# More weight loads under way, no idle products in a stretch of the front, and other keys for the MLP's units in a planned RWKV and MLP kernel

## The chip, the cores and the metric

The kernel runs on one core of one Trainium2 chip. The metric is the device time of one execution in microseconds (us); the median of the runs counts. The core has five engines with an instruction queue each: TensorE (PE) for products and transposes, with its weight loads shown apart as PEld, VectorE (DVE), ScalarE (ACT), GpSimd (POOL), and SyncE (SP), which here issues nearly all DMAs.

## The reference

Two stages in fp32. The first is RWKV attention over 4 batches, 8 heads, 768 steps, head size 48:

```
for t in range(S):
    cur = einsum('bhd,bhe->bhde', u * k[t], v[t])
    y[t] = einsum('bhd,bhde->bhe', r[t], state + cur)
    state = w * state + einsum('bhd,bhe->bhde', k[t], v[t])
```

The second takes y as x of 4 x 768 x 384:

```
h  = x.transpose(0, 2, 1) @ U @ V          # over the 768 steps, rank 32
u  = x + h.transpose(0, 2, 1)
out = u + relu(u @ w_ch1) @ w_ch2          # 384 -> 1536 -> 384
```

U, V and both weights reach the chip as 64-bit floats; the kernel reads them as pairs of 32-bit words.

## The kernel before

**Attention.** Each batch is cut into six chunks of 128 steps, n = 0 to 23. A chunk scales k by a table of powers of w (ks, from the table tabf, which is turned by the transposes pt_tabf of back), turns r and k with transposes on PE (ptr, ptk, then rT and kT), makes the score products kT x rT (bank_tr and bank_sc, eight pairs), masks them on DVE (am), and adds am x v and rT x state S into pav. A state product psu gives the next S. dv and dg hold the term with u. Chunks of batch 0 (the front) are cut by `f_scores`, `f_state` and `f_out`; later ones by `a_chunk` or `a_part`.

**MLP.** Behind a batch's attention come the product with U and V (Gs), u in a high and a low part (uTh, uTl), and units of work m_1 and m_2, each for a tile of tokens and a quarter of the 1536 columns. A half-unit is nine products of 128x384 into p: three tiles of weight times high, low and correction parts. m_1 reads w1s and uTh, uTl; ACT makes hh = relu(p) (L1298) and DVE the rest hl (L1299); m_2 reads w2s and hh, hl. The nine products have one line, L384, since a helper records them.

**Weights.** `unit` holds a weight tile: `load` issues its DMA, and converting from 64-bit words takes ACT (L597, L619), DVE (L600, L603) and a split into a high part by ACT (L637) and a low part by DVE or POOL (L638). A list `landing` holds the loads that were made; each load is tied to the landing of the one AHEAD places before it, so that no more than AHEAD are under way. SP issues them in order, and a load that waits holds up what stands behind it.

**The order.** A planner (`Plan`) fixes the order on every engine. Each step has a key, given by `at(t, f)`: the front's chunks stand EACH = 4.5 apart, the MLP's units PER apart from T0 on, the blocks of later batches by begin[b]. The planner walks through the steps by keys with a model of each operation's time, its engine and the readiness of its inputs, and always starts the best one next. Its PE part reckons with half or full clock (`clock`). Where PE would stand idle in plan time, it puts in idle products ident x ident of 128x128 into the bank wake (`woken`, line 384 in the profile), the number of which comes from the model. Prices are given with each operation, such as 950 ns for the score products and 500 for the outer ones.

The lines that the change touches in the load:

```
big_one = len(parts) == 1 and name != "u"
before = landing[-AHEAD] if big_one and len(landing) >= AHEAD else None
...
tc.add_manual_dep(mine[0].ins, before[0][0].ins.name, ...)
```

and the place at which idle products are put in:

```
until = t - 150 - (...)
while self.pe_end(x, begin.ways[0][1], 0, False) < until:
    self.woken.append((x, filler))
```

Of the kernel before, what the change touches and what calls it, by code (L numbers as in the profile page):

```python
# [47 lines left out]
class Plan:  # L48
# [19 lines left out]
    USED = 0.36  # L68

    BACKLOG = 0.3  # L70
    NEXT = 1500
    YIELD, YIELDS, NEAR = 2, 140000, 100

# [47 lines left out]
    def clock(self, t):  # L121
        w = int(t // self.WINDOW)
        for x in range(len(self.clocks), w + 1):
            self.clocks[x] = 1.0 if self.work.get(x - 1, 0) > self.USED * self.WINDOW else 0.5
        return self.clocks[w]

    def pe_end(self, t, ns, share, note=True):
# [27 lines left out]
    def schedule(self):  # L155
# [50 lines left out]
        while left:  # L206
# [36 lines left out]
                cands[w[0]] = [c for c in cands[w[0]] if c[0] is not o]  # L243
            if e == "PE":
                for begin, end, filler in self.wakes:
                    if begin.end is None or end.end is not None:
                        continue

                    x = free[e]
                    until = t - 150 - (min(self.SPARE * (t - x), 600) if self.clock(x) == 1 else 0)  # L250
                    while self.pe_end(x, begin.ways[0][1], 0, False) < until:
                        self.woken.append((x, filler))
                        x = self.pe_end(x, begin.ways[0][1], 0.8)
                        tiled = False
                    t = max(t, x)
                if o.tiled != tiled:
                    t, tiled = t + self.MODE, o.tiled
                ns = self.pe_end(t, ns, 0.65 if tiled else 0.85) - t
# [61 lines left out]
def rwkv_moe(ctx: ExitStack, tc: tile.TileContext, r, k, v, w, u, U, V, w1, w2, out):  # L320
# [65 lines left out]
    def pe(ns, fn, w_, r_, tiled=False, dk=0.0):  # L386
        return op("PE", ns, fn, w_, r_, tiled=tiled, dk=dk)
# [154 lines left out]

    wide = U.dtype == I64

    AHEAD = 3
    HOLD = 6
    landing = []

# [366 lines left out]
    def in_turn(*lists):  # L915
        for k_ in range(max(map(len, lists))):
            for l in lists:
                if k_ < len(l):
                    l[k_]()
# [74 lines left out]
    def f_scores(n):  # L994

        rT, kT = trs[n]
        abs_[n] = [bank(t, f"pab_{n}_{j}") for j, t in enumerate(AB)]

        def product(q, j):
            rows = head_rows(j)  # L1000
            return nc.tensor.matmul(abs_[n][j].t[:, q * C:(q + 1) * C], lhsT=kT.t[rows, q, :], rhs=rT.t[rows, q, :],  # L1001
                                    start=True, stop=True)
        pe(950, lambda: in_turn(*([lambda q=q, j=j: product(q, j) for q in range(NP)] for j in range(2))), abs_[n], [rT, kT],
           tiled=True)
        ams[n] = []
        for j in range(2):
            am = xbuf([128, NP, C], F32, "bl", 5, f"am_{n}_{j}")
            ams[n].append(am)
            on_dve(512, lambda e, am=am, j=j: e.tensor_tensor(am.t, abs_[n][j].t.rearrange("p (q t) -> p q t", q=NP),
                                                              before_.unsqueeze(1).broadcast_to([128, NP, C]), ALU.mult),  # L1010
                   [am], [abs_[n][j]])
# [32 lines left out]
    def f_out(n):  # L1044

        vt, vb = vs[n]
        rT = trs[n][0]
        avp[n] = [bank(t, f"pav_{n}_{j}") for j, t in enumerate(("av", "mm"))]

        def inner(q, j, i):  # L1050
            return nc.tensor.matmul(avp[n][j].t[i * C2:(i + 1) * C2, q * D:(q + 1) * D],  # L1051
                                    lhsT=ams[n][j].t[:, q, i * C2:(i + 1) * C2], rhs=vt()[:, 2 * q + j, :],
                                    start=(q == 0), stop=(not n and q == NP - 1), skip_group_check=True)

        def outer(q, j, i):
            rows = head_rows(j)
            return nc.tensor.matmul(avp[n][j].t[i * C2:(i + 1) * C2, q * D:(q + 1) * D], lhsT=rT.t[rows, q, i * C2:(i + 1) * C2],  # L1057
                                    rhs=St[n, 0].t[rows, q, :], start=False, stop=(q == NP - 1), skip_group_check=True)
        for j in range(2):
            pe(500, lambda j=j: in_turn(*([lambda q=q, i=i: inner(q, j, i) for q in range(NP)] for i in range(2))),  # L1060
               [avp[n][j]], [ams[n][j], *vb], tiled=True)
        if n:
            pe(500, lambda: in_turn(*([lambda q=q, j=j, i=i: outer(q, j, i) for q in range(NP)] for i in range(2) for j in range(2))),
               avp[n], [rT, St[n, 0]], tiled=True)
        x = xs[n] = xbuf([128, DM], F32, "x", NX, f"x_{n}")
        dv = dvs[n]
        for j in range(2):
            def pair(ap, j=j):
                return ap.rearrange("p (q j) d -> p q j d", j=2)[:, :, j]
            on_dve(192, lambda e, j=j, pair=pair: e.tensor_tensor(  # L1070
                pair(by_head(x.t)), avp[n][j].t[:, :NP * D].rearrange("p (q d) -> p q d", q=NP), pair(dv.t), ALU.add),
                [(x, j)], [avp[n][j], dv])
# [388 lines left out]
    def at(t, f):  # L1461
        steps.append((t, len(steps), f))

    T0, PER = 40.0, 1.85
    UV, GX, UVC = -84.9, (3, 33.0), (25.0, 33.0)
    EARLY, LEAD = 4, 12.0
    FRONT, EACH = 9.0, 4.5
# [41 lines left out]
    def attention(b, t0, per, lead, step):  # L1509
        n0 = b * NCH  # L1510
        for c in range(NCH):
            n = n0 + c
            t = t0 + per * c
            prepare(n, t - per - lead if c else t - 2 * lead)
            if front(n):
                at(t - SC, lambda n=n: f_scores(n))
                at(t - SU_, lambda n=n: f_state(n))
                at(t, lambda n=n: f_out(n))
                at(t - 1, lambda n=n: a_dg(n))
                if c >= GX[0]:  # L1520
                    at(max(t + per - 0.05, GX[1] + 0.1 * c), lambda n=n: gx.append(c_gx(*(range(n + 1) if n == GX[0] else [n]))))
                continue
            if c == 0:
                at(t - 5, lambda n=n: a_first(n))
            if merged(n):
                at(t, lambda n=n: a_chunk(n))
            else:
                at(t, lambda n=n: a_part(n, 0))
                at(t + per / 2, lambda n=n: a_part(n, 1))
            at(t - 0.1, lambda n=n: a_dg(n))  # L1530
        return t0 + per * NCH
# [4 lines left out]
    for b in range(B):  # L1536
        n0 = b * NCH
        last = b + 1 == B
        t = begin[b]
        if b:  # L1540
            t0, per = ((begin[b - 1] + 34, 8.0), (begin[b - 1] + 5, 10.0))[b > 1]
            for c in range(NCH):
                at(t0 + per * c - per - 16, lambda n=n0 + c: a_load(n))
            for c in range(0, NCH, 3):
                if turned(n0 + c):
                    continue
                for i in (1, 3, 0, 2):
                    at(t0 + per * c - per - 18 + 0.1 * i, lambda n=n0 + c, i=i: (a_load_blocks(n, i, 0), a_load_blocks(n, i, 1)))
            end = attention(b, t0, per, 5.0, 0)
        at(end, lambda b=b: c_g(b))  # L1550
        if b == 0:
            at(end + 0.9, lambda: again.append(pe(220, refill, [wk2], [xs[NCH - 1], V3])))
            at(end + 1, lambda: c_xu(0, 0))
            at(end + 1.5, lambda: again.append(pe(0, lambda: None, [wk2], [(uT[0, 0][1], NCT - 1)])))
            for i in range(TPB):
                at(t + 2 + 0.1 * i, lambda i=i: c_x(0, 1, i))
            at(t + 3, lambda: c_xu(0, 1))
        else:
            if inside(b, 0):
                for i in range(3):  # L1560
                    at(end + 0.1 + 0.1 * i, lambda b=b, i=i: c_x(b, 0, i))
                at(end + 1, lambda b=b: c_xu(b, 0))
            else:
                for i in range(TPB):
                    at(end + 0.2 + 0.1 * i, lambda b=b, i=i: (c_u(b, i), c_store(b, i)))
                for ct in range(NCT):
                    at(end + 1 + 0.1 * ct, lambda b=b, ct=ct: c_blocks(b, 0, ct))
                    at(end + 5 + ct, lambda b=b, ct=ct: c_turn(b, 0, ct))
            for i in (3, 4, 5):
                at(end + (8 if b > 1 else 2) + 0.3 * (i % 3), lambda b=b, i=i: (c_u(b, i), c_store(b, i, parts=2 if b > 1 and i > 3 else 1)))  # L1570
        for ct in range(NCT if b else 0):
            at(t + 2 + ct, lambda b=b, ct=ct: c_blocks(b, 1, ct))
            at(t + 16 + ct, lambda b=b, ct=ct: c_turn(b, 1, ct))
        for j, f in enumerate(mlp_units(b)):
            at(t + PER * j, f)
# [42 lines left out]
```

## Time and profile before

| what | value |
|---|---|
| median of 3 runs | 403.54 us (403.44 to 403.96) |
| the profiled execution | 403.42 us |
| its span, first to last instruction | 401.7 us |
| granted clock of PE, mean | 0.996 |
| PE busy | 393.9 us, 98% |
| DVE, ACT, POOL busy | 262.6, 139.2, 100.3 us |
| products p of 128x384 | 1728 |
| MB moved by DMA | 45.28 |

The span is what the trace covers; 1.72 us of the execution lie outside it. The share of busy time is an average over stages. In the front (up to about 36 us) all engines work on batch 0's attention; from 42 us the MLP's products fill PE, with blocks of later batches' attention between them; from 309 us on there is nothing but the MLP. A row with several instructions shows them as one ("x4"), with the time from the first's start to the last's end.

### The profile page before, as it was taken

The numbers are of one execution on the slowest core, as the hardware profiler recorded it, in microseconds if no ns is written. First come the engines' busy times: TensorE is split into PE (matmuls) and PEld (weight loads), VectorE is DVE, ScalarE is ACT, GpSimd is POOL, SyncE is SP. The second block draws the span as 40 slices with busy tenths as digits, with TensorE's granted clock in tenths as the row PEclk, the third lists the DMA queues.
The fourth block names the chain that finished last, engine by engine and source line by source line (L and its number), as shares of the span: only waits on it lengthen the run. The fifth ranks groups of instructions, "written<-read, shape, count | busy, mean of one in ns | idle before, by whom it ended". The sixth has DMA issues, their size and how long they took to land.

```text
span 401.7 us, 11702 instructions
## 1 busy us (share of the span) xinstructions
PE 393.9 (98%) x4872; PEld 380.4 (95%) x4872; DVE 262.6 (65%) x559; ACT 139.2 (35%) x376; POOL 100.3 (25%) x147
## 2 busy tenths in 40 slices
PE   7999999999999999999999999999999999999994
PEld 7888999999999999999999999999999999999994
DVE  4789998899999868976784596776424552121122
ACT  3688869437361332222112331202112221111110
POOL 2881223266736042231230150431000110000000
PEclk9999999999999999999999999999999999999998
DMA  9988699879578586864786858310104620001001
GB/s 150 178 231 237 118 270 182 192 181 220 88 120 193 82 184 104 164 101 82 146 156 98 188 117 143 75 19 12 51 2 74 145 77 2 0 0 62 2 0 64
DMA packets 189994, 45.28 MB, mean 113 GB/s; under 512 B 174701, under 2 KB 188398, under 8 KB 189934
## 3 DMA queue, kind: packets, MB, share of 16 engines
q1 hardware_dynamic: 186382, 43.28, 53.0%
q10 hardware_dynamic: 3552, 1.18, 1.3%
q8 instruction: 40, 0.66, 0.7%
q14 instruction: 20, 0.16, 0.1%
HBM read 36.77 MB, written 7.67 MB: 111 GB/s over the span
## 4 chain that ended last, share of the span: by engine, by line
PE 94%; DVE 3%; DMA 1%; SPq 0%; issue 0%; ACT 0%
PE p L384 75%; PE pav L898 2%; PE pav L904 2%; PE bank_tr L1001 2%; PE pav L1051 2%; DMA ld<-in_r_dram 1%; PE bank_tr L858 1%; PE bank_sc L858 1%; PE ptr L807 1%; PE pav L883 1%; PE bank_tr L872 1%; PE bank_tr L1165 1%; PE bank_sc L872 1%; PE pav L1057 1%; PE psu L1023 1%; PE bank_tr L807 1%
## 5 line engine op out<-in xcount | busy, mean ns | idle before, releaser
L384 PE MATMUL p<-uTh,w1s 128*128 128x384 f32 x576 | 148.6, 338 | 0.0
L384 PE MATMUL p<-w2s,hh 128*128 128x384 f32 x576 | 119.1, 337 | 0.1
L1298 ACT ACTIVATE hh<-p 128x384 fp32r<-128x384 f32 x96 | 47.1, 490 | 207.3 <-PE p L384 206.7
L1299 DVE SCALAR_TENSOR_TENSOR hl<-p,hh 128x384 fp32r<-128x384 f32 x96 | 53.2, 554 | 93.3 <-ACT hh L1298 92.2
L384 PEld LDWEIGHTS p<-uTh,w1s 128*128 128x128 f32 x576 | 103.1, 188 | 1.1 <-DVE w1s L638 0.3
L384 PEld LDWEIGHTS p<-w2s,hh 128*128 128x128 f32 x576 | 100.8, 188 | 1.1 <-DVE w2s L638 0.4
L384 PE MATMUL p<-uTl,w1s 128*128 128x384 f32 x288 | 96.6, 335 | 0.0
L384 PE MATMUL p<-w2s,hl 128*128 128x384 f32 x288 | 66.7, 335 | 0.0
L384 PEld LDWEIGHTS p<-uTl,w1s 128*128 128x128 f32 x288 | 54.0, 188 | 0.2 <-DVE uTl L1229 0.2
L384 PEld LDWEIGHTS p<-w2s,hl 128*128 128x128 f32 x288 | 51.5, 188 | 0.0
L1275 POOL TENSOR_TENSOR uTl<-ut,uTh 128x384 fp32r<-128x384 f32 x8 | 8.1, 1018 | 74.9 <-ACT uTh L1274 74.8
L759 POOL MEMSET ks<- 128x128 f32 x24 | 4.7, 205 | 66.1 <-PE bank_tr L872 65.3
L898 PE MATMUL pav<-ldv,am 64*64 64x48 f32 x288 | 20.2, 219 | 0.0
L904 PE MATMUL pav<-S,rT 48*64 48x48 f32 x528 | 19.6, 218 | 0.0
L898 PE MATMUL pav<-vsw,am 64*64 64x48 f32 x288 | 18.4, 218 | 0.0
L898 PEld LDWEIGHTS pav<-ldv,am 64*64 64x64 f32 x288 | 17.9, 134 | 0.0
L904 PEld LDWEIGHTS pav<-S,rT 48*64 48x64 f32 x528 | 17.9, 135 | 0.0
L1339 DVE TENSOR_TENSOR x<-p,x 128x384 f32<-128x384 f32 x30 | 14.9, 548 | 3.6 <-PE p L384 3.3
L898 PEld LDWEIGHTS pav<-vsw,am 64*64 64x64 f32 x288 | 17.2, 134 | 0.0
L597 ACT ACTIVATE raw_w<-raw_w 128x384 int32<-128x384 uint8 x23 | 13.1, 569 | 8.7 <-DMA raw_w<-in_moe_w_ch_dram 8.7
L796 POOL TENSOR_TENSOR kT<-kT,tabT 112x512 f32<-112x512 f32 x10 | 12.9, 1290 | 11.8 <-DVE kT L794 6.3
L769 POOL TENSOR_TENSOR dv<-ldr,ldk 128x384 f32<-128x384 f32 x14 | 14.2, 1016 | 5.6 <-DVE x L1103 3.0
(189 smaller groups left out, 593.8 us busy)
## 6 DMA issues: line engine op xcount, KB each, us to landing
raw_w<-in_moe_w_ch_dram SPq DMA_DIRECT2D x24, 384.0 KB, 5.0
out_dram<-x SPq DMA_DIRECT2D x21, 192.0 KB, 2.2
ldr<-in_r_dram SPq DMA_DIRECT2D x20, 192.0 KB, 3.3
ldk<-in_k_dram SPq DMA_DIRECT2D x20, 192.0 KB, 3.8
ldv<-in_v_dram SPq DMA_DIRECT2D x20, 192.0 KB, 4.0
bl<-in_r_dram SPq DMA_DIRECT2D x79, 48.0 KB, 2.4
bl<-in_k_dram SPq DMA_DIRECT2D x79, 48.0 KB, 2.4
ub<-ud SPq DMA_DIRECT2D x15, 192.0 KB, 2.9
```

The lines of the kernel that those rows point to most:

```text
L384: return nc.tensor.matmul(*args, **kw)
L597: nc.scalar.activation(word(0), byte(), AF.Copy, scale=7.49 / 255)
L769: on_either(384, lambda e, a_=a_, b_=b_: e.tensor_mul(dv.t, a_()[:, :, :D], b_()[:, :, :D]), w_, r_, only="POOL" if front(n) else None)
L796: on_either(512, lambda e: e.tensor_mul(subs(xT.t[:PD]), subs(xT.t[:PD]), table(i)), [xT], [tabT])
L807: nc.tensor.transpose(pt.t[:PD, q * C:(q + 1) * C], src().rearrange("p h d -> p (h d)")[:, q * PE_:q * PE_ + PD], ident_)
L858: return [lambda q=q, i=i: nc.tensor.matmul(pt.t[(i ^ j) * C2:(i ^ j) * C2 + C2, q * C2:(q + 1) * C2], lhsT=kT.t[rows, q, i * C2:(i + 1) * ...
L898: return nc.tensor.matmul(to(q, j, i), lhsT=am[j].t[half, q, :], rhs=vsw[n].t[half, q, :] if j else vt()[half, 2 * q, :], start=((i == 1 i ...
L904: return nc.tensor.matmul(to(q, row, i), lhsT=rT.t[rows, q, i * C2:(i + 1) * C2], rhs=St[n, i].t[rows, q, :], start=False, stop=((alone or ...
L1275: on_either(384, lambda e: e.tensor_tensor(ul.t[:, ct, :], ut.t, f32(uh.t[:, ct, :]), ALU.subtract), [(ul, ct)], [ut, (uh, ct)])
L1298: on_act(384, lambda: nc.scalar.activation(hh.t, pt.t[:, :TB], AF.Relu), [hh], [pt])
L1299: on_dve(384, lambda e: e.scalar_tensor_tensor(hl.t, pt.t[:, :TB], 0.0, f32(hh.t), ALU.max, ALU.subtract), [hl], [pt, hh])
L1339: on_dve(384, lambda e, x=x, pt=pt: e.tensor_tensor(x.t, pt.t[:, :DM], x.t, ALU.add), [x], [pt])
```

## The change

Six edits, all to numbers or conditions of the planner but for the first:

- AHEAD goes from 3 to 5: five weight loads may be under way.
- A new QUIET = 7000, 9500: where plan time lies between these, no idle products are put in.
- `clock` counts on the full clock from its third step on, whatever the work before.
- The score products are priced at 1000 instead of 950, the outer products at 520 instead of 500.
- PER goes from 1.85 to 1.95: the units of the MLP have keys further apart.
- The diagonal dg of the front's chunks has its key at t - 0.1 instead of t - 1, and the blocks of batches 2 and 3 begin at begin[b - 1] + 6 instead of + 5.

```
+    QUIET = 7000, 9500
...
-            self.clocks[x] = 1.0 if self.work.get(x - 1, 0) > self.USED * self.WINDOW else 0.5
+            self.clocks[x] = 1.0 if x > 1 or self.work.get(x - 1, 0) > self.USED * self.WINDOW else 0.5
...
-                    if begin.end is None or end.end is not None:
+                    if begin.end is None or end.end is not None or self.QUIET[0] < t < self.QUIET[1]:
...
-    AHEAD = 3
+    AHEAD = 5
...
-        pe(950, lambda: in_turn(*([lambda q=q, j=j: product(q, j) for q in range(NP)] for j in range(2))), abs_[n], [rT, kT],
+        pe(1000, lambda: in_turn(*([lambda q=q, j=j: product(q, j) for q in range(NP)] for j in range(2))), abs_[n], [rT, kT],
...
-            pe(500, lambda: in_turn(*([lambda q=q, j=j, i=i: outer(q, j, i) for q in range(NP)] for i in range(2) for j in range(2))),
+            pe(520, lambda: in_turn(*([lambda q=q, j=j, i=i: outer(q, j, i) for q in range(NP)] for i in range(2) for j in range(2))),
...
-    T0, PER = 40.0, 1.85
+    T0, PER = 40.0, 1.95
...
-                at(t - 1, lambda n=n: a_dg(n))
+                at(t - 0.1, lambda n=n: a_dg(n) )
...
-            t0, per = ((begin[b - 1] + 34, 8.0), (begin[b - 1] + 5, 10.0))[b > 1]
+            t0, per = ((begin[b - 1] + 34, 8.0), (begin[b - 1] + 6, 10.0))[b > 1]
```

A line more stands in the changed kernel from line 71 on, so its numbers are one higher. On PE, the order near the start of the program, where the first chunk is turned and its scores are made, is in the kernel before:

```order
L384 MATMUL wake<-ident 128x128
L807 MATMUL ptr_138<-ident,ld_93 112x128 x4
L384 MATMUL wake<-ident 128x128 x2
L488 MATMUL pt_tabf<-ident,back 128x112 x4
L384 MATMUL wake<-ident 128x128
L1001 MATMUL bank_tr<-rT_160,kT_150 128x128
L1001 MATMUL bank_sc<-rT_160,kT_150 128x128
```

and in the changed one:

```order
L385 MATMUL wake<-ident 128x128
L808 MATMUL ptr_138<-ident,ld_93 112x128 x4
L489 MATMUL pt_tabf<-ident,back 128x112 x4
L1002 MATMUL bank_tr<-rT_158,kT_149 128x128
L1002 MATMUL bank_sc<-rT_158,kT_149 128x128
L1002 MATMUL bank_tr<-rT_158,kT_149 128x128
```

Three idle products are gone, two ahead of pt_tabf and one ahead of the scores. Over the whole program PE has no other instruction more or less; behind the first chunk the two orders are alike up to about 63 us of the trace before, as are those of DVE, ACT and POOL up to about 52 us.

On SP, the first weight loads, with the semaphores that each waits for (a load of DMAHW1 to DMAHW7 is tied to the landing of an earlier one on that semaphore; w1_0 is the first quarter of w_ch1), before:

```order
L572 DMA raw_w1_0_497<-in_moe_w_ch1_dram 128x3x256 [waits DMAHW1_49]
L572 DMA raw_w2_0_503<-in_moe_w_ch2_dram 128x768 [waits DMAHW2_49]
L572 DMA raw_w1_1_505<-in_moe_w_ch1_dram 128x3x256 [waits DMAHW3_49]
L572 DMA raw_w2_1_599<-in_moe_w_ch2_dram 128x768 [waits DMAHW4_49,DMAHW1_49]
L572 DMA raw_w1_2_615<-in_moe_w_ch1_dram 128x3x256 [waits DMAHW5_49,DMAHW2_49]
L572 DMA raw_w1_3_647<-in_moe_w_ch1_dram 128x3x256 [waits DMAHW6_49,DMAHW3_49]
```

and in the changed kernel:

```order
L573 DMA raw_w1_0_486<-in_moe_w_ch1_dram 128x3x256 [waits DMAHW1_49]
L573 DMA raw_w2_0_500<-in_moe_w_ch2_dram 128x768 [waits DMAHW2_49]
L573 DMA raw_w1_1_502<-in_moe_w_ch1_dram 128x3x256 [waits DMAHW3_49]
L573 DMA raw_w2_1_511<-in_moe_w_ch2_dram 128x768 [waits DMAHW4_49]
L573 DMA raw_w1_2_528<-in_moe_w_ch1_dram 128x3x256 [waits DMAHW5_49]
L573 DMA raw_w1_3_589<-in_moe_w_ch1_dram 128x3x256 [waits DMAHW6_49,DMAHW1_49]
```

The second semaphore is gone from the fourth and fifth load, and the sixth waits for the first.

On DVE, late in the conversion of the weights, between the last low part of a weight (w2s_11) and a rest hl of the MLP (hl_0_1_8, batch 0, second tile of tokens), before:

```order
L638 TENSOR_TENSOR w2s_11_2248<-raw_w2_11_1737,w2s_11_2248 128x384
L1299 SCALAR_TENSOR_TENSOR hl_0_0_11_2261<-p1_0_0_11_2221,hh_0_0_11_2252 128x384
L794 STREAM_TRANSPOSE rT_13_2265<-bl_12_0_1454 128x256
L794 STREAM_TRANSPOSE rT_13_2265<-bl_12_2_2018 128x256
L794 STREAM_TRANSPOSE kT_12_2065<-bl_12_3_2105 128x256
L794 STREAM_TRANSPOSE kT_13_2239<-bl_12_3_2105 128x256
L760 TENSOR_TENSOR ks_12_2215<-ldk_12_2241,tab_922 128x8x48
L1299 SCALAR_TENSOR_TENSOR hl_0_1_8_2296<-p1_0_1_8_2244,hh_0_1_8_2287 128x384
```

and in the changed kernel:

```order
L639 TENSOR_TENSOR w2s_11_2239<-raw_w2_11_1720,w2s_11_2239 128x384
L797 TENSOR_TENSOR rT_13_2237<-rT_13_2237,tabT_900 112x512
L1300 SCALAR_TENSOR_TENSOR hl_0_0_11_2291<-p1_0_0_11_2226,hh_0_0_11_2286 128x384
L795 STREAM_TRANSPOSE rT_14_2295<-bl_12_0_1622 128x256
L795 STREAM_TRANSPOSE kT_12_2198<-bl_12_3_2151 128x256
L795 STREAM_TRANSPOSE kT_13_2230<-bl_12_3_2151 128x256
L797 TENSOR_TENSOR kT_12_2198<-kT_12_2198,tabT_900 112x512
L761 TENSOR_TENSOR ks_12_2204<-ldk_12_2241,tab_919 128x8x48
L770 TENSOR_TENSOR dv_12_2322<-ldr_12_2232,ldk_12_2241 128x384
L797 TENSOR_TENSOR kT_13_2230<-kT_13_2230,tabT_900 112x512
L770 TENSOR_TENSOR dv_12_2322<-dv_12_2322,ub_136 128x384
L1300 SCALAR_TENSOR_TENSOR hl_0_1_8_2339<-p1_0_1_8_2310,hh_0_1_8_2332 128x384
```

Four more rows stand between the two: three products with the table tabT and two for dv came from POOL, one transposition went elsewhere. Over the whole program DVE has six rows more, 720 for 714.

## Rows read from the trace of the kernel before

**Rows 1.** The page's first part: busy time of each engine, its share of the span and its instructions; and the second part's line of DVE, the busy share in tenths of 40 slices.

```profile
PE 393.9 (98%) x4872; PEld 380.4 (95%) x4872; DVE 262.6 (65%) x559; ACT 139.2 (35%) x376; POOL 100.3 (25%) x147
...
DVE  4789998899999868976784596776424552121122
```

**Rows 2.** The windows: each stretch in us, then its length, the busy us of PE, PEld, DVE, ACT and POOL with the instructions, then the granted clock, the share of DMA and GB/s.

```profile
9.70:13.10 3.40, 3.40 (x72) 3.09 (x70) 2.95 (x6) 1.30 (x5) 2.51 (x3) 1.00 1.09 208
...
36.00:42.00 6.00, 5.66 (x42) 4.83 (x43) 5.45 (x12) 5.17 (x14) 1.02 (x1) 1.00 0.82 166
42.00:52.00 10.00, 9.91 (x56) 8.98 (x55) 10.00 (x23) 8.06 (x18) 2.80 (x7) 1.00 0.70 129
52.00:96.00 44.00, 44.00 (x539) 42.84 (x538) 39.52 (x86) 27.66 (x72) 19.13 (x25) 1.00 0.89 204
96.00:134.00 38.00, 38.00 (x658) 36.27 (x657) 37.22 (x78) 16.66 (x51) 18.82 (x22) 1.00 0.74 143
...
309.00:396.50 87.50, 87.49 (x505) 87.16 (x503) 27.17 (x48) 16.14 (x34) 3.02 (x3) 1.00 0.15 39
```

**Rows 3.** The chain of work that ended last, in order of time: start us, us, what.

```profile
49.82 1.85 PE p L384 x9
...
79.29 3.33 PE p L384 x18
82.62 0.44 PE bank_tr L807 x4
83.05 1.57 PE p L384 x9
84.62 0.44 PE bank_tr L807 x4
...
309.09 87.41 PE p L384 x504
```

**Rows 4.** What PE waited for between 13 and 52 us: us in total, times, longest us.

```profile
PE pu L384 <- DVE Gs L1188: 0.3, 1, 0.3
```

**Rows 5.** The timeline of the front: start us, us, engine, line, operation, out<-in, and in brackets the idle time before.

```profile
6.22 1.10 PE L807 MATMUL ptr<-ident,ld 128*112 128x128 f32 x4 [0.31 <-DMA ld<-in_r_dram]
...
6.64 0.62 ACT L508 COPY back<-pw 112x512 f32<-112x512 f32 x1 [3.46 <-DVE pw L503]
...
7.12 1.06 PE L384 MATMUL wake<-ident 128*128 128x128 f32 x4
...
7.36 1.13 DVE L820 SCALAR_TENSOR_TENSOR rT<-ptr,wif,pw 112x128 f32<-112x128 f32 x4
...
7.97 0.95 PE L488 MATMUL pt_tabf<-ident,back 112*128 112x112 f32 x4
...
8.72 0.66 PE L384 MATMUL wake<-ident 128*128 128x128 f32 x2
8.96 0.48 ACT L490 COPY tabf<-pt_tabf 128x384 f32<-128x384 f32 x1 [1.61 <-PE pt_tabf L488]
...
9.31 0.57 PE L1001 MATMUL bank_tr<-rT,kT 48*128 48x128 f32 x1
...
9.68 0.31 PE L1001 MATMUL bank_tr<-rT,kT 48*128 48x128 f32 x1
...
9.83 0.27 PE L1001 MATMUL bank_tr<-rT,kT 48*128 48x128 f32 x1
...
10.39 0.27 PE L1001 MATMUL bank_tr<-rT,kT 48*128 48x128 f32 x1
...
10.60 0.65 PE L807 MATMUL ptr<-ident,ld 128*112 128x128 f32 x4
10.70 0.69 DVE L1009 TENSOR_TENSOR am<-bank_tr,before 128x512 f32<-128x512 f32 x1 [0.20 <-PE bank_sc L1001]
```

**Rows 6.** The timeline where the next idle products stand, behind the second chunk's scores.

```profile
14.72 1.28 PE L384 MATMUL wake<-ident 128*128 128x128 f32 x10
14.74 1.00 POOL L760 TENSOR_TENSOR ks<-ld,tabf 128x384 f32<-128x384 f32 x1
...
15.84 0.61 PE L807 MATMUL ptk<-ident,ks 128*112 128x128 f32 x4
```

**Rows 7.** The first weight loads: the timeline's row of SP, the DMA issues of 23 to 26 us and of 28 to 33.5 us (number, KB each, median us from issue to landing), and the timeline's rows of ACT for the first and the fourth conversion.

```profile
23.80 9.71 SPq L572 DMA_DIRECT2D raw_w<-in_moe_w_ch_dram  x8
...
raw_w<-in_moe_w_ch_dram SPq DMA_DIRECT2D x3, 384.0 KB, 5.3
...
raw_w<-in_moe_w_ch_dram SPq DMA_DIRECT2D x5, 384.0 KB, 4.3
...
30.70 0.57 ACT L597 ACTIVATE raw_w<-raw_w 128x384 int32<-128x384 uint8 x1
...
33.41 0.59 ACT L597 ACTIVATE raw_w<-raw_w 128x384 int32<-128x384 uint8 x1
```

**Rows 8.** Groups of DVE instructions by line over the whole span: busy us, mean ns of one, idle time before.

```profile
L794 DVE STREAM_TRANSPOSE kT<-bl 128x256 f32<-128x256 f32 x30 | 12.6, 426 | 0.8 <-DMA bl<-in_k_dram 0.8
...
L769 DVE TENSOR_TENSOR dv<-dv,ub 128x384 f32<-128x384 f32 x14 | 10.0, 718 | 0.0
...
L796 DVE TENSOR_TENSOR kT<-kT,tabT 112x512 f32<-112x512 f32 x5 | 3.3, 668 | 0.0
L769 DVE TENSOR_TENSOR dv<-ldr,ldk 128x384 f32<-128x384 f32 x6 | 3.3, 542 | 0.0
```

## The prediction

> **What bounds the kernel now.** I read the page's shares first: TensorE (PE) is busy 393.9 of 401.7 us, VectorE (DVE) 262.6 [rows 1]. The windows then say where the rest lies [rows 2]: from 52 us to the end of the products PE has no idle time that a row shows (44.00 of 44, 38.00 of 38, 87.49 of 87.50), while the stretches 36 to 42 and 42 to 52 leave 0.34 and 0.09 idle, with DVE busy 10.00 of 10 in the second. The chain of waits gives PE's pace [rows 3]: nine products of 128x384 take 1.57 us, and the last 504 take 87.41, 0.173 each; a group of transposes between two units (82.62 + 0.44 = 83.06) leaves no gap. One piece at 49.82 takes 1.85 for nine, 0.28 over the pace. The waits of PE name one other, 0.3 us on Gs [rows 4]. So behind 52 us the time is PE's own work. An edit can gain by less work on PE, by an earlier arrival at 52 us, or by a better pace in the front; it loses by a new wait behind 52 us.
>
> The front is read from the timeline [rows 5]. Four transposes take 1.10 us at 6.22 and 0.65 at 10.60, and eight pairs of score products start 0.37 apart at first and 0.11 apart from 9.83: PE runs at the lower of its two levels until about 9.7 us and at the higher one after it. The granted clock reads 1.00 (2.4 GHz) over the stretch, so the durations are what I go by.
>
> **The idle products that go.** In the order they are one row of two ahead of pt_tabf and one ahead of the scores; the trace shows each product as two rows. pt_tabf needs back, which ACT ends at 6.64 + 0.62 = 7.26, and PE is through with ptr at 6.22 + 1.10 = 7.32; it starts at 7.97, behind the four idle rows from 7.12 [rows 5]. Without them it starts at about 7.31, 0.66 earlier, and tabf with it (8.96 to 8.30). The scores need rT, which ends at 7.36 + 1.13 = 8.49, and start at 9.31 behind two idle rows from 8.72; without these they start at about 8.55, since pt_tabf then ends at 7.31 + 0.95 = 8.26. That is 0.76 earlier, but they run at the lower level for longer. I keep the moment of the step at 9.7, take twice the 0.11 for a pair ahead of it and 0.37 for the first: pairs start at 8.55, 8.92, 9.14, 9.36, 9.58, then 9.76, 9.87, 9.98 in place of 10.39. The gain at the last pair is 10.39 - 9.98 = 0.41, with the rounding of a pair 0.42. The next ptr starts 0.21 behind it (10.60 to 10.18), am on DVE at 10.28 for 10.70.
>
> Does the 0.42 get through? At 14.72 five idle products follow, which stay in both orders; they end at 15.84, when ks (14.74 + 1.00 = 15.74 on POOL) is just there [rows 6]. POOL's ks hangs on the table tabf, which comes 0.66 earlier, so PE's own order decides there, and the shift stays. From there to about 52 us the orders of PE, DVE, ACT and POOL are the same in both programs; the DVE work of 37 to 52 us starts when PE delivers, so it shifts with PE. Behind 52 us PE has nothing to wait for, so the shift goes to the end. **Term: -0.42 us.** Bounds: 0 (if the front gives it back at 14.72) and -0.76 (if the step of the clock moves with the scores).
>
> A rule that speaks against this edit is weighed as a rival below.
>
> **Five loads instead of three.** In the order the fourth and fifth weight load no longer wait for the first and second; SP is free earlier. In the trace SP spends 23.80 to 33.51 on eight weight loads [rows 7]; the first three land 5.3 us after issue, the five later ones 4.3. ACT converts the first at 30.70 and the fourth at 33.41. The conversion of a weight is in DVE's and ACT's fixed orders, which are full by then (DVE 5.45 of 6 and 10.00 of 10 [rows 2]), so a load that lands earlier starts nothing earlier: **0**. Bounds: a gain of all that PE waits in 36 to 52 us, 0.34 + 0.09 + 0.28 = 0.71; a loss if five loads share what three had: 5.3 x 5 / 3 = 8.8, the first lands at 23.80 + 8.8 = 32.6, against 30.70 at which ACT takes it, 1.9 late. Loads 4 to 8, with up to three under way, land in 4.3, not later than the first three; so I stay at 0.
>
> **Units further apart in the order; scores and outer products priced higher; diagonals and batches moved.** These set keys and prices of the planner and add no work on PE. Counted over the order, PE has the same instructions but for the idle products. What changes: blocks of attention of batch 1 stand one to three half-units of 1.57 us earlier among the MLP's, and DVE has six instructions more (taken from POOL and ACT). On PE a unit moved past transposes costs 0 [rows 3]. On DVE, at the place shown in the order behind w2s_11, hl_0_1_8 has four rows more ahead of it: three multiplications of kT or rT at 0.67, dv at 0.54 and at 0.72, less one transposition at 0.43: 2.0 + 1.26 - 0.43 = 2.8 us [rows 8]. Over 52 to 134 us DVE is idle 4.48 + 0.78 = 5.26 us [rows 2], so the sum of the work fits, and PE does not wait unless one product's hl comes late. **0**, bounds 0 and +2.8 (rival C).
>
> **The sum** is made against the profiled execution, 403.42 us (span 401.7 and 1.72 around it), which is 0.12 below the median of 403.54: 403.42 - 0.42 + 0 + 0 = **403.0**. Two tenths of a per cent, 0.81 us, is about what a measurement of this kernel can tell from no change: faster is below 402.73, slower above 404.35.
>
> **Rivals.**
>
> B, the step of the clock comes later. Between 6.22 and 9.31 the idle products are all that PE did besides transposes [rows 5]. Without them PE does transposes, waits some 0.3 us from 8.26 to 8.55, and then scores. If the step then comes only behind the first chunk, the stretch 9.7 to 13.1, in which PE is busy 3.40 of 3.40 [rows 2], runs at half the pace and costs 1.7 us: 403.42 - 0.42 + 1.7 = 404.7. If it comes half-way, 0.85 less 0.42 gives 403.9. For it: transposes ran at 1.10 a group from 6.22 without lifting the pace before 9.7. Against it: PE still has work from 6.22 to 8.26 and from 8.55 on, and stands only for those 0.3 us. The Trainium skill, page "TensorE: Matmul & The Clock Gate", section "Part 4: PE-mode transpose", says that a transpose does not count as busy PE as another product does and that the full clock does not engage for it. By that rule the products taken out are the ones that count and this rival, 404.7, would be the forecast; the 1.10 us at 6.22 agree with it, the 0.65 at 10.60 behind the step do not tell. It decides from the point at which the first score products no longer run at 0.11 apart from 9.8 on.
>
> C, DVE falls behind. hl_0_1_8 is late by the 2.8 us of new work ahead of it, less what DVE was ahead. Over 96 to 134 us DVE is already busy 37.22 of 38, so the 0.78 left don't take 2.8; the cover is DVE's lead on PE, which the rows don't show. With a lead of one unit, 1.57 us, PE waits 2.8 - 1.57 = 1.2 (404.2); with none it waits 2.8 (405.8); I put it near the first, at 1.5: 404.5. Against it: the 4.48 idle from 52 to 96 us can be used first, since blocks stand earlier. It decides when DVE's lead is under 2.8 us.
>
> D, the weights set PE's waits at 36 to 52 us. If ACT or DVE waits for a load where I see only order, 0.71 goes too: 403.0 - 0.7 = 402.3. Against it: DVE 10.00 of 10.
>
> E, the five loads share the queues and the first weight comes up to 1.9 us late: 403.0 + 1.9 = 404.9 at most.
>
> **How the numbers follow.** The forecast (403.0, from 402.6 if the whole 0.76 comes through to 403.5 if nothing does) has 0.53, of which 0.08 lies under 402.73. B has 0.20: 0.12 at 404.7, 0.08 near 403.9. C 0.12, of which 0.08 above 404.35. D 0.10, all faster. E 0.05. Faster 0.08 + 0.10 = 0.18; slower 0.12 + 0.08 + 0.05 = 0.25; within 0.2%: 0.57. The range 402.4 to 404.7 leaves out half of D, a part of B's far case and what C and E hold above it, some 0.17.
>
> **What would show it.** Right: pt_tabf near 7.3, scores near 8.55, the next ptr near 10.2, am near 10.3, ptk of ks near 15.4, the last 504 products again at 0.173 and starting 0.4 earlier than 309.09; the fourth and fifth weight load issued with the first three; no wait of PE behind 52 us. B: pairs of scores at 0.2 apart behind 9.8 us. C: a wait of PE on hl between 96 and 134. D: nine products at 49.8 in 1.57. E: ACT's first conversion later than 30.3. I am wrong altogether if the last 504 products start at another time than 308.7 by over half a us, for a reason that is none of these.

## The result

The changed kernel is slower: a median of 406.91 us (404.86 to 409.47, 7 runs) against 403.44 (402.51 to 403.96, 7 runs), a ratio of 1.0086 with a 95% interval of 1.0062 to 1.0110. The forecast of 403.0 had the wrong sign, and its range ended at 404.7.

The profiled execution of the changed kernel took 409.47 us with a span of 407.7; it is the longest of its seven, 6.0 us over the span before, so what follows is the account of a bad execution; the median lost 3.5 us. PE's busy time barely grew:

```profile
PE 395.9 (97%) x4866; PEld 381.4 (94%) x4866; DVE 263.3 (65%) x565; ACT 143.2 (35%) x389; POOL 89.3 (22%) x136
```

The windows, with the columns of [rows 2], show where PE now stands: 1.11 us in 36 to 42 (the 0.34 before were a wait on Gs, which here falls in 42 to 52), 2.26 in 52 to 96 (none before) and 0.28 in 96 to 134.

```profile
9.70:13.10 3.40, 3.40 (x33) 2.82 (x33) 2.23 (x4) 0.70 (x3) 2.94 (x3) 1.00 1.12 212
...
36.00:42.00 6.00, 4.89 (x84) 4.03 (x79) 4.19 (x10) 3.54 (x11) 1.02 (x1) 1.00 0.46 89
42.00:52.00 10.00, 9.67 (x58) 9.03 (x57) 9.91 (x23) 9.10 (x21) 2.80 (x7) 1.00 0.69 115
52.00:96.00 44.00, 41.74 (x521) 39.79 (x520) 40.84 (x87) 28.12 (x70) 14.69 (x20) 1.00 0.88 211
96.00:134.00 38.00, 37.72 (x614) 36.15 (x613) 35.92 (x78) 21.05 (x67) 14.38 (x17) 1.00 0.68 130
```

In the stretch 9.7 to 13.1 PE is as busy as before, but gets through 33 instructions instead of 72: it runs at half the pace. The granted clock of the row reads 1.00 all the same: the trace's first record of that clock starts at 14.70 us here and at 9.75 us in the kernel before, and what lies ahead of the first record counts as 1.00. So in the front the durations decide. The timeline of the front shows it, to be read against [rows 5].

```profile
6.62 1.10 PE L808 MATMUL ptr<-ident,ld 128*112 128x128 f32 x4 [0.71 <-DMA ld<-in_r_dram]
...
7.51 0.95 PE L489 MATMUL pt_tabf<-ident,back 112*128 112x112 f32 x4
...
8.39 0.58 PE L1002 MATMUL bank_tr<-rT,kT 48*128 48x128 f32 x1
...
10.05 0.42 PE L1002 MATMUL bank_tr<-rT,kT 48*128 48x128 f32 x1
...
10.40 1.10 PE L808 MATMUL ptr<-ident,ld 128*112 128x128 f32 x4
...
15.11 0.27 PE L1002 MATMUL bank_tr<-rT,kT 48*128 48x128 f32 x1
...
15.22 0.27 PE L1002 MATMUL bank_tr<-rT,kT 48*128 48x128 f32 x1
...
15.99 0.65 PE L808 MATMUL ptr<-ident,ld 128*112 128x128 f32 x4
...
16.47 1.28 PE L385 MATMUL wake<-ident 128*128 128x128 f32 x10
```

The scores do start earlier (8.39 for 9.31), yet the transposes at 10.40 still take 1.10, the eight pairs are 0.21 apart from the second on, and 0.11 apart only in the next chunk, from 15.11. The five idle products that both kernels keep start at 16.47 for 14.72 [rows 6]: 1.75 us lost where 0.42 were to be gained.

Then the chain of waits names two stops, one at 36.64 and one ahead of 93.94, and the same rows as [rows 3] elsewhere.

```profile
36.64 1.10 issue
37.74 0.56 PE pav L1052 x13
...
52.73 1.86 PE p L385 x9
...
93.61 0.33 issue
93.94 4.87 PE p L385 x27
...
313.45 88.96 PE p L385 x513
```

The waits of PE behind 52 us, and those of its weight loads (PEld) from 80 to 100 us, columns as in [rows 4]:

```profile
PE p L385 <- DVE rT L795: 2.2, 1, 2.2
PE p L385 <- DVE hl L1300: 0.3, 1, 0.3
```

```profile
PEld p L385 <- issue: 2.3, 1, 2.3
```

PE lists the stop ahead of 93.94 under a DVE row that ended near its end, PEld under nothing ("issue"). In the program this product waits for DVE only as far as hl_0_1_7, which ended at 89.3, so the DVE row is the neighbour in time and not the cause. Both stops are followed by plain work; each comes just behind a transfer on the DMA queue named "instruction". The DMA view, for 34 to 35.2 us and for 35.2 to 36.7 (packets, MB, share of 16 engines' time):

```profile
q1 hardware_dynamic: 614, 0.41, 106.2%
```

```profile
q1 hardware_dynamic: 1287, 0.30, 89.9%
q8 instruction: 1, 0.02, 4.6%
```

In the first stretch the engines are full and there is no packet of instructions; the packet comes in the second, and PE goes on at 37.74. From 91.3 to 92.6 us there is one such packet too, ahead of the restart at 93.94. The two packets end at 36.44 and 92.40, 1.30 and 1.54 us before PE goes on. Added up: 1.75 in the front, 1.10 and 2.17 at the stops, 0.28 on hl near 130 us, 5.3 of the 6.0.

### The profile page after: what moved, and what is told of

It reads as the page before. It is cut to its first block, busy times and chain, and to the rows that moved or that the text cites. A ratio compares the mean times of both kernels' runs of the same rounds, so it can differ in the third digit from the quotient of the medians.

```text
span 407.7 us, 11678 instructions
## 1 busy us (share of the span) xinstructions
PE 395.9 (97%) x4866; PEld 381.4 (94%) x4866; DVE 263.3 (65%) x565; ACT 143.2 (35%) x389; POOL 89.3 (22%) x136
## 4 chain that ended last, share of the span: by engine, by line
PE 87%; DVE 7%; DMA 2%; ACT 1%; issue 1%; POOL 0%; SPq 0%; DVEq 0%
PE p L385 69%; PE pav L899 2%; PE bank_tr L1002 2%; PE pav L1052 2%; PE pav L905 1%; DMA ld<-in_r_dram 1%; PE ptr L808 1%; PE bank_tr L859 1%; PE bank_sc L859 1%; DVE raw_w L601 1%; PE bank_tr L1166 1%; PE psu L1024 1%; PE pav L884 1%; PE bank_tr L873 1%; PE pav L1058 1%; PE bank_sc L873 1%
## 5 line engine op out<-in xcount | busy, mean ns | idle before, releaser
L1151 ACT ACTIVATE SW<-S,wm 112x48 f32<-112x48 f32 x52 | 13.2, 324 | 16.7 <-DVE S L1138 15.7
L1138 DVE TENSOR_TENSOR S<-bank_tr,SW 112x192 f32<-112x192 f32 x15 | 5.3, 357 | 13.4 <-PE bank_tr L873 13.4
```

The source lines that it names most:

```text
L1151: nc.scalar.activation(dec.t[:, q], new.t[:, q], AF.Copy, scale=wm.t[:, q])
```

## The experiments

The theories were these. Theory 1: without the idle products TensorE's step to the higher level comes late. Theory 2: five weight loads fill the DMA queues, PE's instructions are fetched late, and PE stands. The rival: the new order of the units makes DVE late, and PE waits for it. Putting the idle products back into the changed kernel leaves the order on all engines as it is, and the number of loads under way was changed without touching the planner, so that each part could be moved alone. Ratios are to the kernel before, run on the same chip in the same series.

| run | idle products ahead of the scores | loads under way | order | ratio (95% interval) | wait of PE put down to issue, 33 to 38 us |
|---|---|---|---|---|---|
| changed kernel | 6 | 5 | new | 1.0086 (1.0062 to 1.0110) | 1.10 |
| idle_back | 9 | 5 | new | 1.0045 (1.0026 to 1.0064) | 1.52 |
| three_loads | 6 | 3 | new | 1.0030 (1.0013 to 1.0047) | none |
| both_back | 9 | 3 | new | 1.0001 (0.9984 to 1.0019) | none |
| before_no_idle | 6 | 3 | before | 1.0015 (0.9996 to 1.0035) | none |
| before_few_idle | 1 | 3 | before | 1.0032 (1.0008 to 1.0056) | none |
| before_two | 9 | 2 | before | 1.0126 (1.0081 to 1.0171) | 0.46 |
| before_four | 9 | 4 | before | 1.0002 (0.9976 to 1.0027) | 0.98 |
| before_five | 9 | 5 | before | 1.0072 (1.0046 to 1.0099) | 1.53 |
| before_eight | 9 | 8 | before | 1.0087 (1.0053 to 1.0121) | 1.34 |
| first_five | 9 | 5, then 3 | before | 1.0062 (1.0037 to 1.0088) | 0.52 |
| before_more_idle | 11 | 3 | before | 0.9986 (0.9967 to 1.0005) | none |
| more_idle_again | 11 | 3 | before | 1.0004 (0.9982 to 1.0027) | none |
| five_idle | 13 | 3 | before | 1.0003 (0.9982 to 1.0024) | none |
| new_order_best | 11 | 3 | new | 1.0004 (0.9982 to 1.0026) | none |

The idle products are counted from the first instruction to the first scores. The table's last column is from one profile of each.

**The parts of the change, undone one by one.** idle_back:

```
-    QUIET = 7000, 9500
+    QUIET = 0, 0
```

> The changed kernel with the three idle products of the front put back, and every engine's order otherwise as in the changed kernel. Theory 1 (without them the step of TensorE's clock comes late): score pairs are 0.11 apart again behind 9.8 us, the front ends about 1.7 earlier, and the time is about 405.2 for 406.9. Theory 2 (five weight loads hold up something else) leaves two thirds of the loss here, at least 1.5 over the kernel before. Rival (the new order makes DVE late, the idle products don't matter): 406.9, no change.

three_loads, which leaves the planner's own count at five and ties each load to the third one ahead of it:

```
+            held = landing[-3] if big_one and len(landing) >= 3 else None
...
-                    if before:
-                        tc.add_manual_dep(mine[0].ins, before[0][0].ins.name,
+                    if held:
+                        tc.add_manual_dep(mine[0].ins, held[0][0].ins.name,
```

> The changed kernel, its order kept, with three weight loads under way instead of five. Theory 2 (PE's waits of 1.1 us at 36.6 and 2.2 us at 91.8, put down to issue, come from five loads filling the DMA queues ahead of PE's instruction fetch): both waits are gone, the time is 1.5 to 3.3 less, about 404 to 405.4; theory 1 leaves the front's 1.7. Rival (the new order of DVE makes PE wait at 91.8): the wait at 91.8 stays and the time is 406 to 407.

both_back has both edits.

> The changed kernel with the idle products back and three loads under way: only the new order is left of the change. Theories 1 and 2 together: 403.2 to 403.9, no waits of PE behind 52 us but 0.3 near 130. Rival (the new order): still 405 to 406.5, with the wait of 2 us near 90.

The three together give the shares. With both undone nothing is left of the loss (1.0001), so the rival falls: the new order of the units, by itself, costs nothing that 12 runs can tell. Idle products back takes 1.0086 to 1.0045, three loads 1.0086 to 1.0030; what either leaves adds up to 0.0075, close to the 0.0086 of both. In us of a 404 us kernel: five loads some 1.8 to 2.3, the missing idle products some 1.2 to 1.7, each about 1 us either way by the intervals. I had expected 405.4 at the most for three_loads and 405.2 for idle_back; 405.47 and 406.01 on a chip whose kernel before ran at 404.33 are at and somewhat over that.

The waits of PE from 13 to 130 us, in idle_back and in three_loads:

```profile
PE pav L1052 <- issue: 1.5, 1, 1.5
PE pu L385 <- DVE Gs L1189: 0.3, 1, 0.3
```

```profile
PE p L385 <- DVE x L1107: 0.7, 1, 0.7
PE pu L385 <- DVE Gs L1190: 0.3, 1, 0.3
```

The wait near 35 us goes with the five loads. The one near 90 us I had expected to go too, but a shorter one stays with three loads (0.7 here, 1.0 in both_back).

**The idle products alone.** before_no_idle leaves them out where the planner had put them:

```
-        todo = [((o.start, o.n), o) for o in self.ops] + [((t, -1), fn) for t, fn in self.woken]
+        todo = [((o.start, o.n), o) for o in self.ops] + [((t, -1), fn) for t, fn in self.woken if not 6500 < t < 8500]
```

> The kernel before without its three idle products ahead of pt_tabf and the scores, its order otherwise kept. Theory 1: the step of the clock comes between 13 and 15 us, the time is 1.3 to 1.8 longer, about 405.0. My forecast's mechanism: pairs at 0.11 behind 9.8, 0.4 shorter, 403.0.

The ratio, 1.0015, is between the two and its interval holds 1. The profile fell on an execution in which the higher level came at about 5 us, ahead of the place of the products left out. The timeline of PE:

```profile
6.06 0.65 PE L807 MATMUL ptr<-ident,ld 128*112 128x128 f32 x4 [0.53 <-DMA ld<-in_r_dram]
```

The transposes take 0.65 at 6.06, as they do at 10.60 in [rows 5]. So the moment of the step differs from one execution to the next by several us, in kernels that are the same up to there.

The same profile shows that an early front is not kept. PE's first product p starts at 41.23 us, 0.78 earlier than in the profile before (42.01), but behind 60 us PE is 0.2 late. The waits from 50 to 60 us:

```profile
ACT raw_w L597 <- DMA raw_w<-in_moe_w_ch_dram: 1.5, 2, 1.1
PEld p L384 <- DVE x L1339: 0.9, 3, 0.4
DVE raw_w L600 <- ACT raw_w L619: 0.8, 2, 0.6
```

ACT waits for two weight loads, DVE for ACT, and the three products of Gs and V start one by one, each behind a row x<-p,x of DVE for which it waits in the program. The profile before has none of these three waits in that stretch.

before_few_idle (`if t > 9000`, one product is left) takes eight out.

> The kernel before, its order kept, without eight of the nine idle products that stand ahead of the first scores. Theory 1 (idle products bring the clock's step forward): the step comes later than without three of them, in most executions behind the first chunk, 1 to 2 us more, 405.3 to 406.3. Rival (the moment of the step is a matter of the single execution, whatever PE did): 403.9 to 404.6.

1.0032, or 1.3 us: outside the noise and smaller than I had expected. Its one profile doesn't show the expected cause: the front ends 0.46 earlier than in the profile before, and the loss is a stop of 1.40 us near 91 us. first_five, below, has all nine idle products, and its profile shows the late step all the same:

```profile
11.28 0.42 PE L1003 MATMUL bank_tr<-rT,kT 48*128 48x128 f32 x1
11.63 1.10 PE L809 MATMUL ptr<-ident,ld 128*112 128x128 f32 x4
15.79 0.37 PE L1003 MATMUL bank_tr<-rT,kT 48*128 48x128 f32 x1
...
16.11 0.27 PE L1003 MATMUL bank_tr<-rT,kT 48*128 48x128 f32 x1
```

The idle products therefore don't secure an early step. That they shift its odds is what the ratios suggest (1.0086 to 1.0045 and 1.0030 to 1.0001 with the three put back, 1.0032 without eight); single profiles can't show odds. The traces' first records of the granted clock start at 9.96 us with one idle product, at 4.99, 13.90 and 14.70 with six, from 5.99 to 15.19 in the eight profiles with nine, and from 5.87 to 7.77 in the four with eleven or thirteen. Three runs tried more of them, two or four ahead of the second transposes (`for _ in range(3 if 5000 < t < 5500 else 1)`, and 5).

> The kernel before, its order kept, with two more idle products ahead of the second group of transposes, where PE waits for a load. Theory 1: the step comes no later, on average a little earlier, 403.8 to 404.3. My forecast's mechanism (idle products only stand in the way): 0.1 to 0.3 more, 404.4 to 404.6.

> The kernel before with two more idle products ahead of the second transposes, a second time, since one series left it open. Theory 1: 0.3 to 0.7 less than the kernel before again, and no execution over 405. Rival (the first series was luck): as the kernel before, with single executions at 405 to 407.

> The kernel before with four more idle products there. Theory 1: the step comes no later than with two more; the products now stand some 0.4 us ahead of transposes whose input has landed, so 403.8 to 404.3. Rival (each idle product only delays): 0.4 to 0.6 over the kernel before.

The first series had no execution over 404.3 and a ratio of 0.9986; the second, of the same kernel, gave 1.0004 and reached 405.77. The first was luck, and five_idle says the same. More idle products than the kernel before has are worth nothing that can be measured. The three profiles say where a gain goes: their first products p start at 41.41, 41.26 and 41.36 us, 0.6 to 0.75 early, and the wait on x near 59 us takes 1.2, 1.7 and 0.3 of it.

**The number of loads alone**, in the order of the kernel before. Each has the edit of three_loads with another number.

> The kernel before, its order kept, with five weight loads under way. Theory 2: a wait of PE of 1.1 to 1.5 us near 33 to 36 us that follows an instruction fetch, and 1.0 to 1.6 more time, about 405.6. Rival (five loads only hurt in the new order): 404.3, no wait there. My forecast's step, a load that lands earlier starts nothing: 404.3.

> The kernel before, its order kept, with eight weight loads under way: the suspected cost enlarged. Theory 2: more waits put down to issue, at least the one near 33 to 36 us and of 1.5 us or more, 405.6 to 408. Rival: 404.3.

> The kernel before, its order kept, with two weight loads under way instead of three. Theory 2 (loads under way hold up PE's instruction fetch): no more waits of PE put down to issue than before, 404.3 or up to 0.5 less, unless weights come late, which would show as a wait of PE on w1s or w2s. Rival (the number of loads doesn't matter, what matters is the order): 404.3.

before_five costs 0.72%, 2.9 us of 404, without any other part of the change. Its chain of waits:

```profile
33.80 0.59 PE pav L1052 x14
34.39 1.53 issue
...
37.99 2.76 PE pv L384 x8
```

and its windows, with the granted clock third from the end:

```profile
34.00:38.00 4.00, 2.47 (x64) 2.02 (x60) 1.83 (x5) 1.88 (x5) 0.00 (x0) 0.89 0.73 170
38.00:42.00 4.00, 4.00 (x25) 3.16 (x26) 2.33 (x6) 1.66 (x6) 1.01 (x1) 0.68 0.69 122
```

PE stands for 1.53 us in the middle of the products of one chunk. Then the granted clock falls from 1.00 to a mean of 0.68 over 38 to 42 us, that is, to the lower level of 1.2 GHz for part of it, and the eight products pv take 2.76; in the kernel before the chain has 1.55 for them. 1.53 + 1.21 is 2.74. This execution is the slowest of the nine (408.35, 4.1 over the median before), so the 2.9 of all nine is not to be split by it. pv releases V, on which DVE's full stretch up to 52 us hangs, so the delay goes through: the first product p starts at 45.22 us for 42.01.

before_eight loses no more than before_five that the intervals could tell, so five already make the loss. before_two is the worst of all, 1.0126, in another way: the weights come late. ACT's waits from 28 to 60 us name them, which the kernel before does not have in that stretch, and PE then waits 0.8 us on V and 1.2 on an x (I had expected the wait on w1s or w2s). Behind the second wait the granted clock is 0.50 over 63 to 66 us. Its stop of 0.46 in the table says that few loads alone don't rule that stop out.

```profile
ACT raw_w L598 <- DMA raw_w<-in_moe_w_ch_dram: 5.2, 3, 2.5
```

> The kernel before, its order kept, with four weight loads under way. Theory 2 as a matter of how much is queued ahead of a fetch: between three and five, 404.5 to 406, with the wait at 33 to 36 us absent or under 1 us. As a matter of the burst alone: as five, 406 to 407.5.

> The kernel before, its order kept, with five loads under way among the first eight weight loads only, three from then on. Theory 2, by what the five loads did so far: the wait put down to issue comes at 33 to 36 us, followed by a stretch at the lower clock where it is near 1.5 us, and costs as much as five throughout, 1.5 to 3 us: 406 to 407.3. Rival (the later loads count as much): 404.8 to 405.5.

first_five puts the loss of the five loads in the first eight (1.0062 of 1.0072). before_four is at 1.0002, though its profile has a wait of 0.98 near 34 us and the fall of the clock behind it. This profile is that of its slowest execution (406.75, five of twelve are below 403.6), so with four the wait seems to come in some executions only, and the median does not show it. The mean granted clock of an execution, which is lower where the clock fell, agrees: it is under 0.995 in six of nine executions with five loads and in five of eight with eight, in one of twelve with four, and in none of the 36 of three_loads, both_back and before_no_idle.

**Where the stops lie.** Whether PE stands for a late input or for late instructions can be told by counting. In the traces, the seven stops near 35 us all lie ahead of PE's 600th row, counted from the start with the idle products, and the five near 90 us all ahead of its 1236th. The windows from 0 to a moment inside a stop show it, in the changed kernel (two), idle_back, new_order_best and before_few_idle, with PE's rows behind its busy time:

```profile
0.00:37.50 37.50, 34.10 (x599) 30.20 (x600) 27.13 (x67) 23.50 (x80) 20.61 (x44) 1.00 0.97 206
0.00:93.50 93.50, 87.70 (x1235) 80.64 (x1236) 80.03 (x180) 62.91 (x176) 37.30 (x70) 1.00 0.89 196
```

```profile
0.00:35.00 35.00, 30.65 (x599) 27.32 (x600) 26.89 (x67) 23.59 (x80) 20.56 (x44) 1.00 0.99 215
```

```profile
0.00:86.60 86.60, 83.28 (x1235) 76.92 (x1235) 76.35 (x170) 61.29 (x172) 34.05 (x65) 1.00 0.91 197
```

```profile
0.00:91.00 91.00, 85.28 (x1235) 77.99 (x1235) 78.78 (x177) 61.80 (x175) 40.07 (x74) 1.00 0.91 197
```

These programs have different numbers of idle products ahead, so the same count is another product: the 1236th row reads uTh and w1s in the changed kernel, hh and w2s in before_few_idle, ldv and ks in new_order_best. A late input would stop PE at the same product; this stops it at the same place in its instructions. And in all twelve cases PE goes on 1.26 to 1.54 us after a packet of 16 KB on the instruction queue has ended, whatever row the waits name. What five loads do to that packet is seen in before and before_five, whose PE rows from 12 to 33.5 us start within 0.02 us of each other: it starts at 31.93 us in the one and at 33.69 in the other. The DMA view, for 31.5 to 33.2 us of before and for 31.5 to 33.4 of before_five:

```profile
q1 hardware_dynamic: 531, 0.53, 95.3%
q8 instruction: 1, 0.02, 3.7%
```

```profile
q1 hardware_dynamic: 509, 0.73, 104.4%
```

In before the packet ends at 32.92 us and the 600th row starts at 34.25, 1.33 later, without a stop: there it is just in time. The DMA engines are near full in both, so their share alone doesn't tell a late packet.

**A better version?** new_order_best has the new order with three loads and eleven idle products.

> The changed kernel's order with three loads under way, the three idle products back and two more ahead of the second transposes. If the order is worth nothing: as the kernel before with two more, 403.7 to 404.0. If it brings PE's wait near 90 us more often (three of its four profiles had one of 0.7 to 2.2): 404.3 to 405.

1.0004: neither this nor any other run beats the kernel before by more than the noise.

## Why the prediction was wrong

- **The bound** was read rightly: behind 52 us PE's pace is as before, 513 products in 88.96 us, 0.173 each. What the sum missed lies ahead of 52 us, and at one point in the middle. But "Behind 52 us PE has nothing to wait for, so the shift goes to the end" was too strong. A front that came 0.78 early lost 0.9 near 59 us in before_no_idle, to weight loads and x; one that came 0.83 early passed there in new_order_best and lost 0.62 at the stop near 87.
- **The idle products, -0.42.** The step that failed is "I keep the moment of the step at 9.7". The arrivals were right: scores at 8.39 (8.55 forecast), pt_tabf at 7.51. But the pairs ran at the lower level to the end, and the front ended 1.75 later. This is rival B. Its net price was 1.28 (1.7 less the 0.42); the profiled front lost 1.75, with the step at 14.70, later than the 13.1 it was priced for. Over many executions the products are worth 1.2 to 1.7 in the new order and 0.6, not clear of noise, in the order of before. I gave it 0.20 because I took the moment of the step in one profile for a property of the kernel. The Trainium skill's rule that a transpose doesn't count as busy PE as another product does (page "TensorE: Matmul & The Clock Gate", section "Part 4: PE-mode transpose") pointed to this side. No run here tests it: in before_no_idle the step came at about 5 us, within the first transposes and ahead of the place of the products left out.
- **Five loads, 0.** The step that failed is "a load that lands earlier starts nothing earlier: 0". As far as it goes it is true: ACT's first conversion of a weight moved with the front, from 30.70 to 32.45. What I left out is who else needs the DMA engines: PE's own instructions, whose packet came 1.76 us later in before_five than in before. Five loads cost 1.8 to 2.9 us. My bound for a loss (rival E, the first weight 1.9 late) was of the right size with the wrong cause, and ACT was not what waited.
- **Keys and prices of the planner, 0.** Right on the whole: both_back is at 1.0001. The wait on hl near 130 us that rival C expected was there with 0.28 instead of 1.2 to 2.8; DVE's lead was larger than one unit.
- **Rival D** did not come: the nine products behind w2s take 1.86 for 1.85 [rows 3]. That ACT and DVE can wait for a weight load, as it supposed, before_no_idle shows near 55 us, where the front is early.
- **The cases were taken as exclusive.** B alone gave 404.7, the loads alone 404.9; together they are near 406.6, outside the range, and the result is near it, in part by luck, since E's 1.9 had another cause. Two edits that act in different places can both go wrong, and the range had no room for it.

What stays open: why the packet ahead of PE's 1236th row comes late more often in the new order. Four of the five profiles of the new order have that stop, of 0.6 to 2.2 us, and one of eleven of the order before (1.40, in before_few_idle). The new order gives something back: nine of the eleven profiles of the order before have a wait of PEld on x near 60 us (0.3 to 2.1 us), and none of the five of the new order has one. That the two cancel fits both_back and new_order_best, which show no loss on average, but no run moved either by itself. Nor did a run delay the instructions by themselves: that they come late is shown by the place of the stops and the start of the packet, and that the loads are what delays them by the runs that change only the loads; how the queues share the engines is not shown.

## What to carry to other kernels

A stall of PE that the waits put down to "issue", in a stretch where the DMA engines are full, calls for a look at the instruction queue in the DMA view, and for a count: where versions with different work ahead stop at the same number of instructions, and not at the same product, the engine waits for its instructions. The engine named in the waits can then be a mere neighbour in time. An early arrival is worth only as much as the next wait leaves of it. Idle products that keep TensorE's clock up can't be costed from one profile, since the moment of the step differs between executions; count on the mean of a dozen runs. When a change has several independent edits, add the losses of the likely failures before the range is set.

## What the hardware showed that I had not expected

A stop of PE of 1.53 us cost 2.74, since the granted clock fell behind it (0.68 over 38 to 42 us in before_five, 0.73 in idle_back and in before_four), while the stops of 1.10 and 2.17 in the changed kernel were not followed by a fall (1.00 in all rows of its windows up to 134 us). In before_four a stop of 0.98 was:

```profile
34.00:38.00 4.00, 3.04 (x56) 2.60 (x56) 2.50 (x7) 2.90 (x7) 0.03 (x1) 0.84 0.99 282
38.00:42.00 4.00, 4.00 (x30) 3.10 (x29) 2.50 (x5) 2.86 (x8) 0.99 (x1) 0.73 0.64 122
```

So the length of the stop alone doesn't tell whether the clock falls. And the step up came as early as before 6.06 us (before_no_idle) and as late as between 12 and 16 (the changed kernel, first_five), in kernels whose first instructions are the same.
